# Shortening the code of a branch that is not taken: an mLSTM cell with a max-out layer behind it

## The chip, the cores and the metric

One NeuronCore of one Trainium2 chip. The metric is the device time of one execution in microseconds, the median of several executions. The kernel before takes 98.31 us (98.18 to 98.48, three runs).

The names of the engines: TensorE is PE in the profile (PEld for its weight loads), VectorE is DVE, ScalarE is ACT, GpSimd is POOL, SyncE is SP; SP issues most of the transfers (67 of 70 in the trace of the kernel before). PSUM is the memory that the matmuls of this kernel write to. The profile counts 16 DMA engines; the last output transfer is carried out in 128 packets of 512 bytes, and its semaphore rises sixteen times, which I read as once for each sixteenth of it (no record names the engine of a packet). A rise that comes long after the others is called a straggler below.

## The reference

Two parts in a row. An attention-like cell with gates (mLSTM), 32 batch-heads of 768 steps with 40 channels:

```python
for t in range(S):
    m_new = np.maximum(f_gate[:, :, t] + m, i_gate[:, :, t])
    f_stab = np.exp(f_gate[:, :, t] + m - m_new)
    i_stab = np.exp(i_gate[:, :, t] - m_new)
    m = m_new
    C = f_stab[:, :, None, None] * C + i_stab[:, :, None, None] * np.einsum('bhd,bhe->bhde', vt, kt)
    n = f_stab[:, :, None] * n + i_stab[:, :, None] * kt
    h_tilde = np.einsum('bhde,bhe->bhd', C, qt)
    nq = np.einsum('bhd,bhd->bh', n, qt)[:, :, None]
    y[:, :, t] = sigmoid(o_gate[:, :, t]) * h_tilde / np.maximum(np.abs(nq), 1.0)
```

Then, with `x` the result as 3072 rows of 320: `out = np.maximum(x @ w1, x @ w2) @ w_out`, with 1024 columns in between.

## The kernel before

The kernel has two ways to the result. The main path is fast and is right only where the gates behave in the usual way; it runs always, and meanwhile it works out a flag that says whether its result holds. If it does not, a general path computes everything anew. For the inputs of the reference the flag is 0.

The end of the main path, cut: the last output tile is split in columns, so that the very last transfer is small, and each piece is copied from PSUM and sent off by SP.

```python
def out_full(u, s, eng=V):
    # ... cut ...
    for po, w in pos[u, s]:
        # ... products into po ...
        cp(eng)(out=o_sb[:, s % 2 if two else 0, :], in_=po)
        if not two:
            SP.dma_start(out=dst[:, 0, w], in_=o_sb[:, 0, :])
```

Then every engine loads the flag and branches:

```python
_, (general,) = nc.values_load_multi_w_load_instructions(
    flag_i[0:1, 0:1], skip_runtime_bounds_check_because="a comparison gives 0 or 1", bass_reorder=False)

with tc.If(general > 0), ExitStack() as gctx:
    # ... cut ...
    with tc.For_i(0, BH, 1) as bh:
        # ... loads; then q and k are transposed one after the other ...
        for n in ("q", "k"):
            xb = gen.tile([128, NT, D], BF, name=f"g_{n}b")
            nc.vector.tensor_copy(out=xb, in_=ld[n])
            pt = pp_f.tile([128, NT, 128], BF, name="g_pt", tag="pf")
            for c in range(NT):
                nc.tensor.transpose(pt[0:D, c, :], xb[:, c, :], ident_b)
        # ... scores in pieces of 384 columns, weights, products ...
    with tc.For_i(0, B, 1) as bb:
        with tc.For_i(0, S, L) as s0:
            # ... load, transpose ...
            with tc.For_i(0, NFF * L, L) as f0:
                # ... up products of one slice of 128 columns ...
            # ... down products, store ...
```

Behind this `If` only the end of the program follows.

## Time and profile before

| | before |
|---|---|
| measured | 98.31 us |
| span of the profiled execution | 97.0 us |
| TensorE busy | 88.8 us |
| last compute instruction ends | 92.83 us |
| last output transfer issued | 92.86 us |
| from that issue to the end of the span | 4.14 us |

The last three rows come from the timeline. I call the last one "the tail" below: it holds the landing of the last transfer and the final barrier, and nothing is computed in it (from 92.9 to 97.0 us every engine is busy for 0.00 us). The lines themselves are shown in the prediction.

### The profile page before, as it was taken

How to read it: one execution, taken by the hardware profiler on the slowest of the kernel's cores; microseconds unless marked ns; L12 is line 12 of the kernel's file. 1: busy time of each engine (PE TensorE's matmuls, PEld its weight loads, DVE VectorE, ACT ScalarE, POOL GpSimd, SP SyncE). 2: the span in 40 equal slices, each digit the busy share in tenths (PEclk: the TensorE clock that was granted, in tenths of full speed). 3: DMA queues.
4: the chain of work that ended last, by engine and by line, in shares of the span. 5: the costliest groups of instructions: out<-in, count | busy, mean ns of one | idle time of the engine just before them, and what ended most of it. 6: DMA issues, size and time to landing. Idle time of an engine off the chain costs nothing.

```text
span 97.0 us, 2280 instructions
## 1 busy us (share of the span) xinstructions
PE 88.8 (92%) x874; PEld 64.8 (67%) x875; DVE 54.8 (57%) x164; ACT 42.4 (44%) x63; POOL 28.1 (29%) x67
## 2 busy tenths in 40 slices
PE   3999979899799999999999999999999999999910
PEld 1346556766488888788777868677776867776800
DVE  4788927952468999597832748962282522223320
ACT  0786693852524780390717085341607053331000
POOL 5054497863654341822244000080000000000000
PEclk9999999999999999999999999999999999999996
DMA  0999999998999889996999999597330120330340
GB/s 12 168 267 330 388 388 371 353 232 128 310 294 234 162 218 362 314 121 112 282 302 136 210 299 232 173 69 178 62 139 0 65 80 4 134 135 10 134 145 4
DMA packets 34049, 18.33 MB, mean 189 GB/s; under 512 B 23152, under 2 KB 31792, under 8 KB 34032
## 3 DMA queue, kind: packets, MB, share of 16 engines
q1 hardware_dynamic: 32594, 17.90, 73.7%
q10 hardware_dynamic: 1438, 0.23, 1.6%
q8 instruction: 8, 0.13, 0.6%
q14 instruction: 9, 0.07, 0.3%
HBM read 12.42 MB, written 3.93 MB: 169 GB/s over the span
## 4 chain that ended last, share of the span: by engine, by line
PE 69%; DMA 16%; SPq 6%; ACT 1%; DVE 1%; issue 1%; DVEq 0%
PE po L510 27%; PE pu L464 18%; DMA ost<-in_o_gate_dram 10%; PE po L506 8%; DMA w<-in_moe_w_dram 6%; PE pu L472 6%; PE ph L357 3%; SPq L118 3%; PE po L494 2%; SPq L104 2%; PE pq L298 2%; PE py L389 1%; SPq L111 1%; ACT ost L267 1%; PE pk L312 1%
## 5 line engine op out<-in xcount | busy, mean ns | idle before, releaser
L481 ACT ACTIVATE gt<-pu 128x1024 bf16<-128x1024 f32 x18 | 17.6, 1021 | 27.3 <-PE pu L472 27.3
L510 PE MATMUL po<-wo,gt 128*128 128x320 bf16 x160 | 26.9, 299 | 0.0
L464 PE MATMUL pu<-xT,wd 128*128 128x256 bf16 (+1 forms) x224 | 24.9, 257 | 1.0 <-POOL wdx L408 0.7
L518 DVE COPY o_sb<-po 128x320 f32<-128x320 f32 (+2 forms) x23 | 10.9, 475 | 20.5 <-PE po L510 20.4
L464 PEld LDWEIGHTS <-wd 128*128 128x128 bf16 x224 | 19.0, 98 | 3.7 <-POOL wdx L408 0.8
L510 PEld LDWEIGHTS <-gt 128*128 128x128 bf16 x160 | 15.0, 98 | 5.2
L367 DVE SCALAR_TENSOR_TENSOR y<-ost,ph 128x320 bf16<-128x320 f32 x20 | 9.6, 482 | 2.5 <-PE ph L357 2.1
L506 PE MATMUL po<-Wc_t,xT 128*128 128x320 bf16 (+2 forms) x50 | 10.7, 296 | 0.0
L267 ACT ACTIVATE ost<-ost 128x320 f32<-128x320 f32 (+2 forms) x14 | 8.7, 658 | 4.2 <-DMA ost<-in_o_gate_dram 4.2
L222 PE MATMUL pd<-warm,ident_b 128*128 128x512 bf16 x24 | 8.7, 484 | 1.7 <-POOL ident_b masks.py:199 1.7
L257 POOL CAST qb<-qst 128x240 bf16<-128x240 f32 (+1 forms) x12 | 5.9, 489 | 12.2 <-DMA qst<-in_q_dram 12.2
L472 PE MATMUL pu<-xT,wd 64*128 64x256 bf16 (+1 forms) x112 | 7.7, 257 | 0.0
L481 ACT ACTIVATE gs<-pu 128x512 bf16<-128x512 f32 x8 | 4.3, 591 | 4.8 <-PE pu L472 4.8
L357 PE MATMUL ph<-cq,qT 120*128 120x123 bf16 (+1 forms) x60 | 6.0, 213 | 0.2 <-DVE qT L299 0.2
L402 POOL TENSOR_TENSOR wd<-w 128x512 bf16<-128x512 f32 x4 | 5.1, 1272 | 2.5 <-DMA w<-in_moe_w_dram 2.3
L357 PEld LDWEIGHTS <-qT 120*128 120x128 bf16 (+1 forms) x60 | 4.5, 98 | 1.9 <-ACT qT L299 0.4
L510 PE MATMUL po<-wo,gs 128*128 128x320 bf16 (+2 forms) x40 | 5.8, 272 | 0.0
L506 PEld LDWEIGHTS <-xT 128*128 128x128 bf16 x50 | 3.9, 98 | 2.8 <-issue 1.8
L472 PEld LDWEIGHTS <-wd 64*128 64x128 bf16 x112 | 4.0, 94 | 2.4 <-issue 1.3
L222 PEld LDWEIGHTS <-ident_b 128*128 128x128 bf16 x25 | 2.5, 116 | 3.7 <-POOL ident_b masks.py:199 1.7
L538 POOL TENSOR_TENSOR a<-i_sb,F 32x640 f32<-32x640 f32 x1 | 1.5, 1528 | 11.2 <-DVE F L536 11.2
L494 PE MATMUL po<-Wc_t,xT 64*128 64x320 bf16 (+2 forms) x25 | 3.6, 292 | 0.5 <-ACT Wc_t L442 0.5
(126 smaller groups left out, 111.7 us busy)
## 6 DMA issues: line engine op xcount, KB each, us to landing
qst<-in_q_dram SPq DMA_DIRECT2D x3, 800.0 KB, 5.9
ost<-in_o_gate_dram SPq DMA_DIRECT2D x3, 800.0 KB
out_dram<-o_sb SPq DMA_DIRECT2D x7, 320.0 KB
w<-in_moe_w_dram SPq DMA_DIRECT2D x8, 256.0 KB, 5.4
out_dram<-o_sb SPq DMA_DIRECT2D x9, 160.0 KB, 3.3
wo_st<-in_moe_w_out_dram SPq DMA_DIRECT2D x2, 640.0 KB
qst<-in_q_dram SPq DMA_DIRECT2D x4, 160.0 KB
wx<-in_moe_w_dram SPq DMA_DIRECT2D x2, 256.0 KB
```

Source lines behind the costliest of these rows:

```text
L222: nc.tensor.matmul(pd[:, 0, :], ident_b, warm, start=True, stop=True)
L257: cp(eng)(out=qp[b % 2][:, c0:c1, 0:2, 0:HS3 * D].rearrange("p c s (h d) -> p c s h d", d=D), in_=qst[b][:, 0:6, c0:c1, :].rearrange("p (s ...
L267: A.activation(out=s, in_=s, func=AF.Tanh, scale=0.5)
L357: nc.tensor.matmul(ph[:, vcols(s), :].rearrange("p a b -> p (a b)"), lhsT, rhs[:, vcols(s), :].rearrange("p a b -> p (a b)"), start=True, ...
L367: V.scalar_tensor_tensor(out=yo, in0=ost[b][:, :, c, :], scalar=1.0, in1=ph[:, :, 0:D], op0=OP.add, op1=OP.mult)
L464: nc.tensor.matmul(pus[i][:, j, :], wd[:, c, f * 128:(f + 1) * 128], x[:, :, GA[i][c], :], start=(c == 0 and (j % 2 == 0 if np_ == 2 else ...
L472: nc.tensor.matmul(pus[i][:, j, :], wd2[r, f * 128:(f + 1) * 128], x[r, :, 2, :], start=False, stop=(j == 3 if np_ == 1 else j % 2 == 1))
L481: A.activation(out=o, in_=pus[i], func=AF.Relu)
L494: nc.tensor.matmul(po, xT[u][r, s // 2, 2, :], Wc_t[r, 2, w], start=True, stop=False)
L506: nc.tensor.matmul(po, x[:, s // 2, GA[s % 2][cc], :], Wc_t[:, cc, w], start=False, stop=False)
L510: nc.tensor.matmul(po, gt[:, f, s % 2, s // 2 * L:(s // 2 + 1) * L], wo[:, f, w], start=False, stop=(f == NFF - 1))
L518: cp(eng)(out=o_sb[:, s % 2 if two else 0, :], in_=po)
```

## The change

The general path's code is made shorter: one loop over 24 output tiles in place of three nested ones, with the up products written out; q and k side by side in one tile, so that one transpose serves both; score products of up to 512 columns in place of 384. The intent, as I read it, is fewer instructions behind the branch. The main path is not touched.

```diff
-            for n in ("q", "k"):
-                xb = gen.tile([128, NT, D], BF, name=f"g_{n}b")
-                nc.vector.tensor_copy(out=xb, in_=ld[n])
-                pt = pp_f.tile([128, NT, 128], BF, name="g_pt", tag="pf")
-                for c in range(NT):
-                    nc.tensor.transpose(pt[0:D, c, :], xb[:, c, :], ident_b)
+            for n, c0 in (("q", 0), ("k", 64)):
+                nc.vector.tensor_copy(out=xb[:, :, c0:c0 + D], in_=ld[n])
+            for c in range(NT):
+                nc.tensor.transpose(pt[0:64 + D, c, :], xb[:, c, :], ident_b)
 # ... cut ...
-                for t0 in (0, HS):
-                    lo = max(t0, j * L)
-                    if lo >= t0 + HS:
-                        continue
-                    n = t0 + HS - lo
+                for lo in range(j * L, S, 512):
+                    n = min(512, S - lo)
 # ... cut ...
-        with tc.For_i(0, B, 1) as bb:
-            with tc.For_i(0, S, L) as s0:
+        with tc.For_i(0, B * NT, 1) as t:
 # ... cut ...
-                with tc.For_i(0, NFF * L, L) as f0:
-                    pu = pp_u.tile([128, L], FP, name="g_pu", tag="pu")
-                    for cc in range(2):
-                        nc.tensor.matmul(pu, wd[:, cc, bass.ds(f0, L)], xg[:, cc, :], start=(cc == 0), stop=False)
+            for f in range(NFF):
+                pu = pp_u.tile([128, L], FP, name="g_pu", tag="pu")
+                for cc in range(2):
+                    nc.tensor.matmul(pu, wd[:, cc, f * 128:(f + 1) * 128], xg[:, cc, :],
+                                     start=(cc == 0), stop=False)
```

More of the change, by code (lines that the diff above doesn't have):

```diff
@@ L764 @@
         M_d = dram.tile([BH, S], FP, name="M_d")
-        x_d = dram.tile([BH, S, D], BF, name="x_d")
+        x_d = dram.tile([B, NT, H, L, D], BF, name="x_d")
         Mg = wst.tile([BH, S], FP, name="Mg", tag="w1")
@@ L771 @@
                 (("q", q), ("k", k), ("v", v), ("o", o_gate))}
-        HS = S // 2
         with tc.For_i(0, BH, 1) as bh:
@@ L782 @@
             nc.gpsimd.dma_start(out=M_b, in_=M_d[bass.ds(bh, 1)].to_broadcast([128, S]))
+            xb = gen.tile([128, NT, 64 + D], BF, name="g_qk")
+            nc.vector.memset(xb, 0.0)
+            pt = pp_f.tile([128, NT, 128], BF, name="g_pt", tag="pf")
             tT = {}
-            for n in ("q", "k"):
-                xb = gen.tile([128, NT, D], BF, name=f"g_{n}b")
-                nc.vector.tensor_copy(out=xb, in_=ld[n])
-                pt = pp_f.tile([128, NT, 128], BF, name="g_pt", tag="pf")
-                for c in range(NT):
-                    nc.tensor.transpose(pt[0:D, c, :], xb[:, c, :], ident_b)
+            for n, c0 in (("q", 0), ("k", 64)):
+                nc.vector.tensor_copy(out=xb[:, :, c0:c0 + D], in_=ld[n])
+            for c in range(NT):
+                nc.tensor.transpose(pt[0:64 + D, c, :], xb[:, c, :], ident_b)
+            for n, c0 in (("q", 0), ("k", 64)):
                 tT[n] = ewp.tile([D, S], BF, name=f"g_{n}T", tag="qT", bufs=2)
-                nc.vector.tensor_copy(out=tT[n], in_=pt[0:D].rearrange("p c t -> p (c t)"))
+                nc.vector.tensor_copy(out=tT[n], in_=pt[c0:c0 + D].rearrange("p c t -> p (c t)"))
             v1 = gen.tile([128, NT, D1], BF, name="g_v1")
@@ L805 @@
                                         channel_multiplier=-1)
-                for t0 in (0, HS):
-                    lo = max(t0, j * L)
-                    if lo >= t0 + HS:
-                        continue
-                    n = t0 + HS - lo
-                    pS = pp_o.tile([128, HS], FP, name="g_pS", tag="po")
+                for lo in range(j * L, S, 512):
+                    n = min(512, S - lo)
+                    pS = pp_o.tile([128, 512], FP, name="g_pS", tag="po")
                     nc.tensor.matmul(pS[:, 0:n], tT["k"][:, j * L:(j + 1) * L], tT["q"][:, lo:lo + n],
@@ L828 @@
             nc.vector.tensor_tensor(out=yy, in0=tt, in1=rc.unsqueeze(2).to_broadcast([128, NT, D]), op=OP.mult)
-            nc.gpsimd.dma_start(out=x_d[bass.ds(bh, 1)].rearrange("o (c p) d -> p (o c) d", p=L), in_=yy)
-        xv = x_d.rearrange("(b h) s d -> b h s d", h=H)
-        ov = out.rearrange("(b s) m -> b s m", b=B)
-        with tc.For_i(0, B, 1) as bb:
-            with tc.For_i(0, S, L) as s0:
-                y = stg.tile([128, DM + 64], BF, name="g_x", tag="qst")
-                nc.gpsimd.dma_start(out=y[:, 0:DM].rearrange("p (h d) -> p h d", d=D),
-                                  in_=xv[bass.ds(bb, 1), :, bass.ds(s0, L), :].rearrange("o h p d -> p (o h) d"))
-                nc.vector.tensor_copy(out=y[:, DM:DM + 64], in_=y[:, DM - 64:DM])
-                px = pp_f.tile([128, 3, L], BF, name="g_px", tag="pf")
-                for cc in range(3):
-                    nc.tensor.transpose(px[:, cc, :], y[:, cc * 128:(cc + 1) * 128], ident_b)
-                xg = stg.tile([128, 3, L], BF, name="g_xT", tag="ost")
-                nc.vector.tensor_copy(out=xg, in_=px)
-                gg = gtp.tile([128, NFF, L], BF, name="g_g", tag="gt")
-                with tc.For_i(0, NFF * L, L) as f0:
-                    pu = pp_u.tile([128, L], FP, name="g_pu", tag="pu")
-                    for cc in range(2):
-                        nc.tensor.matmul(pu, wd[:, cc, bass.ds(f0, L)], xg[:, cc, :], start=(cc == 0), stop=False)
-                    nc.tensor.matmul(pu, wd2[0:64, bass.ds(f0, L)], xg[0:64, 2, :], start=False, stop=True)
-                    nc.scalar.activation(out=gg.rearrange("p f l -> p (f l)")[:, bass.ds(f0, L)], in_=pu, func=AF.Relu)
-                po = pp_o.tile([128, DM], FP, name="g_po", tag="po")
-                for cc in range(3):
-                    r = slice(0, 128 if cc < 2 else 64)
-                    nc.tensor.matmul(po, xg[r, cc, :], Wc_t[r, cc, :], start=(cc == 0), stop=False)
-                for f in range(NFF):
-                    nc.tensor.matmul(po, gg[:, f, :], wo[:, f, :], start=False, stop=(f == NFF - 1))
-                ob = wst.tile([128, DM], FP, name="g_o_sb", tag="wx")
-                nc.vector.tensor_copy(out=ob, in_=po)
-                nc.gpsimd.dma_start(out=ov[bass.ds(bb, 1), bass.ds(s0, L), :].rearrange("o p m -> p (o m)"), in_=ob)
@@ new lines @@
+            nc.gpsimd.dma_start(out=x_d[bass.ds(bh // H, 1), :, bass.ds(bh % H, 1)].rearrange("o c u p d -> p (o c u) d"), in_=yy)
+        xv = x_d.rearrange("b c h p d -> (b c) h p d")
+        ov = out.rearrange("(t p) m -> t p m", p=L)
+        with tc.For_i(0, B * NT, 1) as t:
+            y = stg.tile([128, DM + 64], BF, name="g_x", tag="qst")
+            nc.gpsimd.dma_start(out=y[:, 0:DM].rearrange("p (h d) -> p h d", d=D),
+                              in_=xv[bass.ds(t, 1)].rearrange("o h p d -> p (o h) d"))
+            nc.vector.tensor_copy(out=y[:, DM:DM + 64], in_=y[:, DM - 64:DM])
+            px = pp_f.tile([128, 3, L], BF, name="g_px", tag="pf")
+            for cc in range(3):
+                nc.tensor.transpose(px[:, cc, :], y[:, cc * 128:(cc + 1) * 128], ident_b)
+            xg = stg.tile([128, 3, L], BF, name="g_xT", tag="ost")
+            nc.vector.tensor_copy(out=xg, in_=px)
+            gg = gtp.tile([128, NFF, L], BF, name="g_g", tag="gt")
+            for f in range(NFF):
[3 more added lines that the diff above has]
+                                     start=(cc == 0), stop=False)
+                nc.tensor.matmul(pu, wd2[0:64, f * 128:(f + 1) * 128], xg[0:64, 2, :], start=False, stop=True)
+                nc.scalar.activation(out=gg[:, f, :], in_=pu, func=AF.Relu)
+            po = pp_o.tile([128, DM], FP, name="g_po", tag="po")
+            for cc in range(3):
+                r = slice(0, 128 if cc < 2 else 64)
+                nc.tensor.matmul(po, xg[r, cc, :], Wc_t[r, cc, :], start=(cc == 0), stop=False)
+            for f in range(NFF):
+                nc.tensor.matmul(po, gg[:, f, :], wo[:, f, :], start=False, stop=(f == NFF - 1))
+            ob = wst.tile([128, DM], FP, name="g_o_sb", tag="wx")
+            nc.vector.tensor_copy(out=ob, in_=po)
+            nc.gpsimd.dma_start(out=ov[bass.ds(t, 1)].rearrange("o p m -> p (o m)"), in_=ob)
```

## The prediction

The sum came to 98.31 minus 1.5, which is 96.8 us, and the 1.5 is 95.91 minus 94.40 us of the trace. "Under 0.2 us" in rival 4 stands as a guess.

The account of what a fetch holds and when it comes is estimate. A "block" is the stretch of the program that one fetch is taken to serve. TensorE's next edge, 1982, is 256 on from the seventh fetch. The trace bears that step: read 0.6 or 1.3 us before the fetches at 62.66 and 89.70, 514 to 525 of TensorE's records lie between the two, with one more fetch among them, so 257 to 262 each. The lag behind the five branches was 0.86 to 1.31 us. The edges of the other engines are put at half that step, as their fetches have 8192 bytes against 16384 in the packet records. That a jump to a target behind an edge brings a fetch was assumed as well; pe_1997 and pe_2000 below test it for TensorE.

> **What bounds the kernel now.** The change edits only code under a flag ("the general path"), so I first asked whether that code runs here. The page gives the span (97.0 us of the 98.31 us measured) and what its end hangs on.
>
> ```profile
> span 97.0 us, 2280 instructions
> ...
> PE 88.8 (92%) x874; PEld 64.8 (67%) x875; DVE 54.8 (57%) x164; ACT 42.4 (44%) x63; POOL 28.1 (29%) x67
> ...
> q8 instruction: 8, 0.13, 0.6%
> q14 instruction: 9, 0.07, 0.3%
> ...
> PE 69%; DMA 16%; SPq 6%; ACT 1%; DVE 1%; issue 1%; DVEq 0%
> ```
>
> TensorE is busy for 92% of the span, and the chain is mostly its matmuls. The rows to keep in mind are the two "instruction" queues: instruction fetches are transfers too, 16 KB each on q8 and 8 KB each on q14.
>
> Next, the instructions at the line of the branch (L760) and at the kernel's last line (L884):
>
> ```profile
> L760 POOLq COMPARE_BRANCH  x1: 45/45/45, 78.7 to 78.7; - x1
> L760 ACTq COMPARE_BRANCH  x1: 45/45/45, 86.5 to 86.5; - x1
> L760 PEldq COMPARE_BRANCH  x1: 760/760/760, 91.8 to 91.8; - x1
> L760 DVEq COMPARE_BRANCH  x1: 72/72/72, 92.6 to 92.6; - x1
> L760 SPq COMPARE_BRANCH  x1: 53/53/53, 93.2 to 93.2; - x1
> ...
> L884 SPq EVENT_SEMAPHORE  x14: 17/28/28, 93.8 to 96.9; - x14
> ```
>
> Every engine branches once at L760 and goes on at L884; no row belongs to a line between. The general path never runs: its loops, transposes and products are worth nothing here. What counts is how many instructions each engine jumps over.
>
> Then the chain and the queues at the very end:
>
> ```profile
> 91.28 0.66 PE po L510 x8
> 91.94 0.11 PE po L506 x2
> 92.06 0.46 PE po L510 x8
> 92.52 0.02 issue
> 92.54 0.29 DVE o_sb L518
> ```
>
> ```profile
> q1 hardware_dynamic: 300, 0.17, 14.7%
> q8 instruction: 1, 0.02, 2.0%
> q14 instruction: 2, 0.02, 1.4%
> issues: line engine op xcount, KB each, median us to landing
> out_dram<-o_sb SPq DMA_DIRECT2D x1, 64.0 KB
> ```
>
> The second is the DMA view of 93 to 97 us. Compute ends at 92.83; SP issues the last output transfer (64 KB) at 92.86; the span ends at 97.0. In those 4.1 us no engine computes. And among the output's packets lie three instruction fetches. The trace's packet records put them at 93.38 (16 KB, 1.25 us, q8, TensorE's, as it is the only queue whose fetches follow TensorE's count), 93.94 (8 KB, 0.40 us) and 94.32 (8 KB, 0.49 us), the last two 1.0 to 1.3 us behind the branches of DVE and SP.
>
> The last transfer's semaphore tells what they cost. It rises sixteen times: fourteen rises between 94.25 and 94.40, the others at 95.42 and 95.91. The transfer before it (issued 92.37) has fifteen by 93.99 and the sixteenth at 95.73. On one DMA engine the packets of both stand still until 94.65, that is from 93.38 until the 16 KB fetch is over; on a second until 94.34, the end of the 93.94 fetch. SP passes its waits for the two transfers at 95.75 and 95.93, then 1.07 us of final barrier follow. So the end of this kernel is set by TensorE's instruction fetch in front of one sixteenth of the output.
>
> [...]
>
> **The change part by part.**
>
> Removed and added in the loops: 0 us directly. The tiles of the main path keep their sizes (the score tile grows to 512 columns, but that buffer tag already holds a tile of 512 floats), its order is fixed by hand, and it lies ahead of the general path. I expect its instructions and 92.83 us of compute unchanged.
>
> Moved: the jump's target. From the program listing of the kernel before ([...] branch labels included) the branch and its target stand at: TensorE 1765 to 2011, DVE 205 to 362, ACT 77 to 219, SP 99 to 231, POOL 98 to 272. One loop's frame is 24 to 27 instructions on an engine, and two loops go. TensorE: minus 52 for frames, minus 7 for register work of dynamic slices, minus 12 for six transposes, minus 2 for one product, plus 42 for 24 unrolled up products instead of 3: minus 31, or 41 if ten branch labels count. DVE: minus 50 (60). SP: minus 53 (63). ACT: minus 54 plus 7, about minus 47 (57).
>
> Where do fetch blocks begin? [...] TensorE's fetches lie at 18.97, 31.48, 40.48, 50.32, 62.66, 78.20 and 89.70. Reading its position 0.6 to 1.3 us before each (the lag after the jumps), plus some 35 instructions by which its sequencer leads (the flag's load, number 1764, starts at 91.14 when the matmul of number 1729 is starting), the quiet late ones give 1205 to 1225 for the fifth and 1720 to 1730 for the seventh; 512 apart fits. The seventh block begins near 1726, the next near 1982, give or take 6. DVE: its second fetch (72.52) falls where its sequencer is at 174 to 177, so the next block begins at 302 to 305. SP: its one fetch fits number 73 or 86, next block 201 or 214. ACT: 66 or 74, next 194 or 202.
>
> Before, all targets lie in the next block: 2011 over 1982, 362 over 305, 231 over 214, 219 over 202. [...] After: TensorE 1970 (or, if labels take no room, 1960 against 1979), below; SP 168, well below; ACT 162, below; DVE 302 against 302 to 305 (291 against 299 to 302), below by little. So TensorE's and SP's fetches at the end should vanish, and DVE's probably.
>
> The sum: with none of them the last rise comes with the other fourteen, at about 94.40 instead of 95.91, minus 1.5 us. SP has eight earlier waits to step through, 0.06 us each from 93.75, done at 94.24, so it is there in time: its final wait passes at 94.42 instead of 95.93. The barrier's 1.07 us stays. 98.31 minus 1.5 is 96.8 us.
>
> **The rivals.** (1) Dead code is free: addresses matter to nobody, time 98.3. For it: not one instruction of the change runs. Against it: the two stragglers of sixteen, each behind a fetch. It also comes true if I have misplaced TensorE's block by a dozen instructions, or if the few instructions behind the target (1970 plus 7) and the final barrier still cross into the block: then q8's fetch stays and nothing else helps, since it is the latest. I give this 20%. (2) TensorE's fetch goes but DVE's stays (its target is on the edge): the second straggler, now without SP's fetch beside it, lands at 94.9 to 95.2 rather than 95.42, and the gain is 0.7 to 1.0 us: 97.4 us. Some 28%. (3) The wait moves to SP: its branch costs 0.46 us until the next instruction (93.30 to 93.75), and twelve waits follow. They end at 94.5 at the earliest, so this takes back 0.1 us at most. (4) The fetch moves into the runtime's code behind the kernel and is paid there, inside the 1.3 us that the measured time has over the span. [...] I expect under 0.2 us. (5) Slower: a target just before a boundary, with a block to be fetched while the final barrier waits. Nothing before shows such a stall; 2%.
>
> **Range and chances.** The likely outcomes are 96.8 (about half), 97.4 (over a quarter) and 98.3 (a fifth). I predict 97.0 us, with 96.5 to 98.4 in 8 of 10. Faster by over 2% needs less than 96.34, that is 2.0 us, more than the stragglers cost: 0.10. Within 2%: 0.88. Slower: 0.02.
>
> **What would show it.** Right: the same 2280 or so instructions, compute ending near 92.8; no q8 packet from 93 to 97 us, q8 at 7 packets instead of 8; q14 down by two or three; the last output landing some 1.6 us after its issue instead of 3.05; a span near 95.5. Wrong: q8 still has its fetch near 93.4 (block misplaced); or it is gone and the sixteenth rise is late still (the straggler has another cause); or main-path rows move (addresses or order changed after all).

## The result, and the profile after

The changed kernel takes 97.12 us (97.01 to 97.50, four runs), the kernel before 98.34 us (98.18 to 98.48, four runs). The ratio is 0.9883 (95% interval 0.9852 to 0.9915). Ratios are the mean time of one kernel's fast runs over that of the other's of the same rounds, so not quite the ratio of the medians. The interval says that it is a real gain of a little over 1%.

The page of the changed kernel, span and instruction queues (queue and kind: packets, MB, share):

```profile
span 96.0 us, 2281 instructions
...
PE 89.0 (93%) x875; PEld 65.1 (68%) x875; DVE 54.8 (57%) x164; ACT 42.5 (44%) x63; POOL 28.0 (29%) x67
...
q8 instruction: 7, 0.11, 0.5%
q14 instruction: 6, 0.05, 0.2%
```

One fetch less on q8 (16384 bytes each in the packet records) and three less on q14 (8192 each): besides those of DVE and SP, one at 87.82 that followed ScalarE's branch by 1.27 us and lay ahead of the tail. The work of the engines is the same. (One matmul more, 875 against 874 at 875 weight loads in both, I take for a record that was missing before.) The DMA view of 93 to 97 us:

```profile
q1 hardware_dynamic: 432, 0.33, 24.9%
issues: line engine op xcount, KB each, median us to landing
out_dram<-o_sb SPq DMA_DIRECT2D x1, 96.0 KB
out_dram<-o_sb SPq DMA_DIRECT2D x1, 64.0 KB
```

There is no instruction queue in it. The sixteen rises of the last transfer's semaphore now lie between 1.36 and 1.53 us after its issue, with no straggler; before, the last two came 2.56 and 3.05 us after it. The tail is 2.62 us instead of 4.14, which is 1.52 less.

The branches, and SP's first wait behind its own:

```profile
L760 PEldq COMPARE_BRANCH  x1: 236/236/236, 92.3 to 92.3; - x1
L760 DVEq COMPARE_BRANCH  x1: 72/72/72, 93.1 to 93.1; - x1
L760 SPq COMPARE_BRANCH  x1: 53/53/53, 93.8 to 93.8; - x1
...
L882 SPq EVENT_SEMAPHORE  x14: 17/28/28, 94.0 to 96.0; - x14
```

TensorE's branch took 236 ns instead of 760. Between the end of SP's branch (99 to 172, before to 231) and its next instruction lie 0.14 us instead of 0.46, and on DVE (205 to 305, before to 362) 0.24 instead of 0.50.

Not all of the 1.52 us is seen in the profiled span, which fell by 1.0 only. In this one execution the main path was 0.55 us longer: compute ended at 93.38. Its chain of waits shows where:

```profile
52.98 5.56 DMA ost<-in_o_gate_dram
58.54 0.02 issue
58.56 0.74 ACT ost L267
59.31 0.02 issue
59.33 0.50 DVE y L367
```

A load of the output gate landed late (it was issued 0.47 us later already, at 52.98 against 52.51 before), and TensorE waited 0.44 us for what hangs on it (at 60.26, before the ph product). The other executions of the changed kernel had spans of 95.4 to 95.7 us, and no other trace has compute ending after 93.15 us. It is a variation of the run, not of the change: the main path is the same.

### The profile page after: what moved, and what is told of

It is laid out like the page before. It is cut to its first block, busy times and chain, and to the rows that moved or that the text cites. A ratio compares the mean times of both kernels' runs of the same rounds, so it can differ in the third digit from the quotient of the medians.

```text
span 96.0 us, 2281 instructions
## 1 busy us (share of the span) xinstructions
PE 89.0 (93%) x875; PEld 65.1 (68%) x875; DVE 54.8 (57%) x164; ACT 42.5 (44%) x63; POOL 28.0 (29%) x67
## 3 DMA queue, kind: packets, MB, share of 16 engines
HBM read 12.42 MB, written 3.93 MB: 170 GB/s over the span
## 4 chain that ended last, share of the span: by engine, by line
PE 56%; DMA 23%; SPq 11%; DVE 4%; ACT 2%; issue 1%; DVEq 0%
PE po L510 21%; DMA ost<-in_o_gate_dram 17%; PE pu L464 14%; PE po L506 6%; DMA w<-in_moe_w_dram 6%; PE pu L472 5%; SPq L118 3%; PE ph L357 3%; SPq L380 3%; DVE y L367 2%; PE pq L298 2%; SPq L104 2%; PE po L494 2%; ACT ost L267 2%; PE py L389 1%
```

## The experiments

All targets below are instruction numbers in the program listing, branch labels counted. Padding is done with `drain` instructions, written at the end of the general path, which never run. Where an engine other than TensorE is padded, all targets move by 2 more, as the program gets one block more. All runs gave the right result. The tail and the last rise are from the profiled execution of each run.

| run | targets: TensorE, DVE, SP | fetches in the tail | last rise after issue | tail | time |
|---|---|---|---|---|---|
| before | 2011, 362, 231 | TensorE, DVE, SP | 3.05 us | 4.14 us | 98.34 |
| changed | 1972, 305, 172 | none | 1.53 | 2.62 | 97.12 |
| pe_pad | 2004, 305, 172 | TensorE | 2.47 | 3.55 | 98.05 |
| rest_pad | 1974, 364, 233 | DVE, SP | 2.59 | 3.67 | 98.16 |
| before_pe_cut | 1967, 362, 231 | DVE, SP | 2.58 | 3.66 | 98.37 |
| sp_pad | 1974, 307, 233 | SP | 1.54 | 2.62 | 97.26 |
| dve_pad | 1974, 364, 174 | DVE | 2.57 | 3.65 | 97.99 |
| loops_only | 1986, 304, 172 | none | 1.54 | 2.62 | 96.91 |
| inner_only | 1997, 363, 231 | DVE, SP | 2.51 | 3.59 | 98.25 |
| no_general | no branch | none | 1.52 | 2.51 | 96.86 |
| pe_1990 | 1990, 305, 172 | none | 1.53 | 2.61 | 97.3, one run |
| pe_1994 | 1994, 305, 172 | none | 1.53 | 2.61 | 96.89, one run |
| pe_1997 | 1997, 305, 172 | none | 1.53 | 2.61 | 96.99, one run |
| pe_2000 | 2000, 305, 172 | TensorE | 2.85 | 3.93 | 98.2, one run |

pe_pad, rest_pad, before_pe_cut and sp_pad shared seven runs of the kernel before, 97.90 to 99.01 us with a median of 98.33 (chip 2); the next four, from dve_pad to no_general, shared 97.88 to 98.71 with 98.43 (chip 3). The last four had one run of it, 98.67 (chip 3). The kernel before scatters by about 1 us here, so the times cannot tell half a microsecond from nothing; the tails and the rises can, but they are of one execution each.

### TensorE's fetch alone (pe_pad)

```diff
+        for _ in range(32):
+            nc.tensor.drain()
```

> The changed kernel with 32 never-run instructions added to TensorE's general path alone; its jump target goes from 1972 to 2004, over the block boundary I put near 1982, the other engines stay as in the changed kernel. Theory (TensorE's 16 KB fetch stands in front of the last output packets): one q8 fetch is back between the branch and the end, one of the sixteen completion rises of the last output is late by over 1 us, time 98.2 to 98.5 us, 1.0 to 1.4 us over the changed kernel. Rival A (the gain came from SP's shorter jump) and rival B (it came from the small 8 KB fetches): 97.1 us, as the changed kernel. Rival C (dead code does not matter, the gain is chance): 97.1 too.

Measured 98.05 us, ratio to before 0.9981 (0.9915 to 1.0048). Most of the gain is lost by 32 instructions that never run: the tail is longer by 0.94 us of the 1.52 that the change had won. The DMA view of 93 to 97 us:

```profile
q1 hardware_dynamic: 292, 0.16, 14.0%
q8 instruction: 1, 0.02, 1.5%
issues: line engine op xcount, KB each, median us to landing
out_dram<-o_sb SPq DMA_DIRECT2D x1, 64.0 KB
```

The fetch is back (at 93.06, 0.93 us long), and with it one late rise: 2.47 us after the issue, the others up to 1.53. Rival C falls here, as dead code does matter, and so do A and B as the only cause: SP's jump is as short as in the changed kernel, and no 8 KB fetch is near. The time is 0.15 us below the range that I expected; this fetch took 0.93 us where that of the kernel before took 1.25.

### All others but TensorE (rest_pad), and the mirror of it (before_pe_cut)

```diff
+        for _ in range(57):
+            nc.vector.drain()
+        for _ in range(55):
+            nc.scalar.drain()
+        for _ in range(64):
+            nc.gpsimd.drain()
+        for _ in range(59):
+            nc.sync.drain()
```

> The changed kernel with never-run instructions added to DVE, ACT, GpSimd and SP so that their jump targets are where they were before (364, 221, 274, 233), TensorE's stays below its boundary (1974). Theory: no q8 fetch at the end, q14 fetches of DVE and SP back near 93.9 and 94.3; the straggler behind DVE's fetch costs up to 0.5 to 1.0 us, so 97.5 to 98.0 us, less than all of the gain lost. Rival A (SP's jump stall): 98.3 less what the last transfer hides, at most 97.6. Rival B (8 KB fetches are the cause): 98.3.

The other one takes the kernel before and cuts TensorE's general path only. Its general path would be wrong.

```diff
-                for j in range(c + 1):
+                for j in (c,):
 # ... cut ...
-                                     start=(j == 0), stop=(j == c))
+                                     start=True, stop=(j == c))
 # ... cut ...
-                for f in range(NFF):
+                for f in (NFF - 1,):
```

> The kernel before with 44 never-run instructions cut from TensorE's general path alone (its results would be wrong if it ran; it does not run here), target 1967 instead of 2011; all loops and all other engines as before. Theory: q8 has 7 packets, the latest straggler is gone, the second one (DVE's fetch) stays: last rise near 95.4 instead of 95.9, 97.5 to 98.0 us, as the run with only the other engines padded. Rival A or B: 98.3 as before.

Measured 98.16 us (ratio 0.9964, 0.9909 to 1.0019) and 98.37 us (ratio 0.9998, 0.9941 to 1.0055). Both expectations missed: I had said 97.5 to 98.0. TensorE's fetch is gone in both, and the times show no gain that is clear of the noise; for rest_pad rival B's 98.3 was nearer than my range. The tails are 0.46 and 0.47 us shorter than before, of the 1.52 that all fetches cost. A straggler remains, 2.6 us after the issue, so one of the 8 KB fetches costs about as much as the 16 KB one. My theory was right on the kind and wrong on which fetches matter.

### SP's fetch alone (sp_pad), DVE's alone (dve_pad)

```diff
+        for _ in range(59):
+            nc.sync.drain()
```

> The changed kernel with 59 never-run instructions on SP alone, target 233 as before the change. Theory: SP's 8 KB fetch comes back some 0.5 us after its jump, when nearly all packets of the last output are through; SP's jump takes 0.46 us again, hidden by the landing: 97.1 to 97.4 us. Rival A (SP's jump is what was saved): 98.3, or at least 97.5.

Measured 97.26 us (ratio 0.9885, 0.9826 to 0.9943), as the changed kernel. SP's jump takes 0.46 us again and its fetch is back (the DMA view of 93 to 97 us), and neither costs anything:

```profile
q1 hardware_dynamic: 339, 0.21, 16.7%
q14 instruction: 1, 0.01, 0.8%
```

The fetch lies at 94.44, 1.43 us after the issue, when the output's packets are through (the last starts at 94.19). It comes 1.0 us after the jump, where I had said 0.5.

```diff
+        for _ in range(57):
+            nc.vector.drain()
```

> The changed kernel with 57 never-run instructions on DVE alone, target 364 as before the change. Revised theory (each of TensorE's 16 KB and DVE's 8 KB fetch alone holds back one DMA engine's last packets, the later of the two counts, they do not add): one q14 fetch about 1 us after DVE's branch, one late rise near 2.6 us after the last issue, 98.0 to 98.3 us. Rival (what the four padded engines cost came from SP's longer jump or from two small fetches together): 97.1 to 97.6.

Measured 97.99 us (ratio 0.9961, 0.9919 to 1.0004), at the lower end of the range, and one fetch on q14 as well:

```profile
q1 hardware_dynamic: 372, 0.25, 20.0%
q14 instruction: 1, 0.01, 0.9%
```

The two views look alike; the difference is when. DVE's fetch starts at 94.15, 1.03 us after the issue, while the packets of the last transfer are under way. The packet records show: 120 of its 128 packets of 512 bytes have started by 94.28. The fetch lasts from 94.150 to 94.697. The remaining eight packets, one sixteenth of the transfer, begin at 94.694; the last four of them take 59 to 102 ns each, where the others take 27. Their semaphore packet goes at 95.01 and its rise is recorded at 95.69; the other fifteen are done at 94.66. So one fetch of 8 KB, set off by a jump over code that never runs, costs 1.03 us of tail.

Together with pe_pad this says that the two fetches do not add up: behind each, one rise of the sixteen is late, and only the later counts. TensorE's fetch alone leaves a tail of 3.55 us in pe_pad and of 3.93 in pe_2000 below, DVE's (with SP's or without it) 3.59 to 3.67, both 4.14. The tail goes with the end of the fetch: over the seven runs that have stragglers, eight in all, each one's rise comes 1.0 to 1.3 us after the end of the fetch before it. TensorE's took 0.93 us in pe_pad, but 1.26 in pe_2000 and 1.25 in the kernel before. So the 4.14 us of one execution need not be the usual tail of the kernel before; that may be why the times of before_pe_cut show nothing of its 0.47 us, which is not shown.

### The parts of the change (loops_only, inner_only)

loops_only has the single loop over output tiles and the written-out up products, with the old transposes and score pieces; inner_only has it the other way round.

> Only the loop part of the change (one loop over output tiles, up products unrolled), with the old transposes and products: TensorE's target 1986, DVE's 304, SP's 172. If branch labels take room in the instruction stream, 1986 lies at my block boundary of 1982 give or take 6 and TensorE's fetch probably stays (98.0 to 98.4 us); if they take none, it is 1974 against 1979 give or take 6, and it probably goes (97.0 to 97.3). DVE's fetch is gone in both.

> Only the joint transposes and wider products, with the old loops: TensorE's target 1997, DVE's 363, SP's 231. All fetches stay: 98.2 to 98.4 us, same as before. Rival (the count of instructions as such is what is paid): a little faster, by 14 of 39 TensorE instructions, 97.9.

Measured 96.91 us (ratio 0.9862, 0.9819 to 0.9905) and 98.25 us (ratio 0.9994, 0.9952 to 1.0037). The loops alone bring the whole gain, with the fetches gone, as in the second of the two cases that I had left open. The joint transposes and wider products show none in the times, though the tail of their one profiled execution is 0.54 us shorter. The page of inner_only shows that its 14 instructions less on TensorE did have an effect, which I had not expected:

```profile
q8 instruction: 7, 0.11, 0.5%
q14 instruction: 9, 0.07, 0.3%
```

TensorE's fetch is gone at 1997 already, but DVE's is there (363), and so is the tail of 3.59 us. This run shows again, with the old loops and no padding, that TensorE's fetch was only one of two.

### No branch at all (no_general)

The flag's load, the branch and the general path are taken out. The program is then right for these inputs only.

> The general path and its branch taken out of the program altogether (no longer the same program for other inputs; right for these). Theory: no fetch in the last 4 us in the changed kernel either, so nothing is left to gain but a shorter way of SP, hidden behind the landing: 96.9 to 97.3 us, as the changed kernel. Rival (some cost of the dead code remains, as branch, flag loads or code length): below 96.8.

Measured 96.86 us (ratio 0.9851, 0.9809 to 0.9893), just below the range. Next to loops_only's 96.91 us in the same rounds there is nothing left to gain: the tail is 2.51 us, 0.1 below that of the changed kernel. The rival that a branch or code length still costs something sizeable is out. One thing stays open: the span of no_general is 0.32 us shorter than that of loops_only (94.99 against 95.31), but its time exceeds its span by 1.86 us instead of 1.48, so that nothing of it is seen in the time.

### Where TensorE's block begins (pe_1990, pe_1994, pe_1997, pe_2000)

The padding of pe_pad with 18, 22, 25 and 28 instructions, one profile and one time each.

> The changed kernel with 18 never-run instructions on TensorE, target 1990 (14 branch labels in the stream). If labels take room, the boundary lies between 1997 (no fetch, run inner_only) and 2004 (fetch, run pe_pad): 7 packets on q8, 97 us. If they take none, it lies between 1986 and 2001 in this count: open.

> Target 1994. Labels take room: no fetch at the end, 7 packets on q8, 97 us. Labels take none: the fetch may be back (8 packets, 98 us).

> Target 1997, the same number as in run inner_only, but with 10 labels less ahead of it. Labels take room: no fetch, as there, 97 us. Labels take none: this is 10 instructions further on than there, the fetch is probably back, 98 us.

> Target 2000. Labels take none: fetch, 8 packets on q8, one rise late by 1 us, 98 us. Labels take room: open, the boundary is between 1997 and 2004.

97.3, 96.89, 96.99 and 98.2 us. The pages of pe_1997 and then pe_2000:

```profile
span 95.5 us, 2281 instructions
...
q8 instruction: 7, 0.11, 0.6%
```

```profile
span 96.7 us, 2281 instructions
...
q8 instruction: 8, 0.13, 0.6%
```

Three instructions that never run, and the span is 1.2 us longer. Up to 1997 the tail does not depend on the number of instructions at all (2.61 us at 1990, 1994 and 1997): it is a step. Single runs carry this, whose state is unknown, but the fetch, the late rise and the tail all agree in each. Whether branch labels take room in the stream stays open: the step at 1998 to 2000 with 14 labels and no fetch at 1997 with 24 labels fit both.

No version here beats the changed kernel by more than the scatter of the runs, other than by dropping the general path: loops_only was run in other rounds, and the two have the same tail.

## Why the prediction was right or wrong

**The path is dead: right.** No instruction of the general path is in any trace, and the main path's instructions are the same. The counts behind the branch were nearly right: targets of 1972, 305 and 172 for TensorE, DVE and SP, where I had 1970, 302 and 168.

**An instruction fetch stands in front of one sixteenth of the output: right.** This is what the changed kernel (last rise at 1.53 us), pe_pad (2.47) and dve_pad (2.57, eight packets of 128 held) show, on and off. (A small misreading: on TensorE's side the held packets go on at 94.62 already, at the end of the fetch, not at 94.65.)

**The sum, minus 1.5 us: right in the trace, 1.52 us of tail.** In the measured medians it is 1.22 us: 97.12 us, against the 97.0 that I gave as the middle of several outcomes and the 96.8 for this one. That 97.12 lies so near to 97.0 is in part luck, as 97.0 only stands between the outcomes, and the likeliest of them was 96.8. The changed kernel's profiled run was among its slow ones (a late load); loops_only, with the same tail, gained 1.52 us (98.43 to 96.91).

**"So the end of this kernel is set by TensorE's instruction fetch": only half of it.** It was the later of two stragglers, but the earlier one would have cost nearly as much. In rival 2 I reckoned that DVE's fetch alone would leave 0.7 to 1.0 us of the gain, as its straggler would land at 94.9 to 95.2 without SP's fetch beside it. That term was mis-sized: without SP's fetch it lands just as late, 2.57 us after the issue against 2.56 before. What remains of the gain is 0.46 to 0.54 us in the tails of dve_pad, rest_pad, before_pe_cut and inner_only; in the medians it is 0.44, 0.17, nothing and 0.18 (each against before in its rounds, and within their scatter). I had supposed that SP's fetch added to that delay; sp_pad and dve_pad show that it does not matter.

**Which margin was thin: wrong.** I feared for TensorE, whose block I put near 1982 give or take 6. The step is at 1998 to 2000: 16 to 18 above my figure if labels take room, 7 to 9 if they take none. The figure came from fetch records under load, equal steps between fetches, a guessed lag, and a guessed lead of TensorE's sequencer. So TensorE had some 25 instructions to spare. For DVE I had put the edge at 302 to 305, and the target came out at 305 without a fetch, at 307 in sp_pad too. That edge was not measured, so how narrow it is stays open. My figure had the target at the edge itself (302 against 302 to 305), so that DVE's fetch went is in part luck, and most of the gain hung on it (1.03 us of 1.52 in dve_pad).

**The rivals.** "Dead code is free" is out. SP's waits took nothing back: in the changed kernel the last rise comes at 94.94 and SP passes at 94.96. Nothing moved behind the kernel either: time less span is 1.5 us in both profiled runs. (The 1.3 us that the prediction names sets the median of 98.31 against the span of the one profiled run, which took 98.47.)

**Not settled.** In dve_pad the straggler's rise comes 0.68 us after its semaphore packet, about twice the 0.33 us between the first semaphore packet and the first rise of the others. A third of the 1.03 us that the fetch costs is this excess; the rest is the delay of the packets themselves. No run shows why the rise lags so, or why the held packets are slow. Nor does a trace name the DMA engine; that the fetch and the eight packets share one is read from the times. What a fetch holds is not recorded either. Before the change SP goes on at 93.75 and DVE at 93.12, both ahead of their fetches at 94.32 and 93.94, so they did not wait for these.

## What to carry to other kernels

When the end of a kernel waits for a last transfer, look at what else the DMA engines carry in those microseconds, instruction fetches included, and look at the sixteen rises of its semaphore rather than at the one landing time. In this kernel the gain came when a jump over dead code no longer set off a fetch (tail 4.14 to 2.62 us); a fetch showed no cost in the tail where it came well before the last transfer (ScalarE's, at 87.82: 3.59 us in inner_only, which has it, 3.65 in dve_pad without it) or after it (SP's: 2.62 us in sp_pad and in the changed kernel). Several stragglers of nearly the same size hide each other: with one taken away, about half a microsecond of the 1.52 was won in the tail, and nothing that the times could show; the rest came with the last one.
